# Three groups' product sums in one pair of PSUM banks per stream, with one copy out for the three

## The chip, the cores and the metric

One core of one Trainium2 chip runs the whole program. The metric is the time of the program on the device in microseconds (us); lower is better. The kernel before was timed in three runs: 1245.13, 1245.88 and 1253.26 us, median 1245.88 us.

The engines are TensorE (PE, with its weight loads as PEld), VectorE (DVE), ScalarE (ACT), GpSimd (POOL) and SyncE (SP, which issues the transfers). Each runs its own list of instructions in order, and waits at an instruction until the semaphores named there are reached.

## The reference

`x` holds 4 batches of 12608 rows of 128 numbers. Each batch is first attended to by 32 learned points, then each row attends to those 32 results, and each row goes through a small network with 1024 hidden units. All is fp32.

```python
h = mab(I, x)                       # per batch: 32 points look at all rows
x = mab(x, h)                       # each row looks at the 32 results
h = x @ w_in                        # 128 -> 1024
e = exp(h - max(h)); sm = e / (sum(e) + 1e-09)
solu = h * sm
ln = (solu - mean(solu)) / sqrt(var(solu) + 1e-06) * g_ln
out = ln @ w_out                    # 1024 -> 128
```

## The kernel before, in words

**Tiles, groups, super groups.** A batch is cut into 99 tiles of 128 rows (the last one has 64). Four tiles make a group (`GS`), so a batch has 25 groups, the last of three tiles. Three groups make a super group (`FG`), so a batch has nine: eight of three groups and one of a single group. In all there are 396 tiles, 100 groups and 36 super groups.

**The path of a tile.** PE multiplies the tile's attention weights into `h` (L946, two PSUM buffers `h0` and `h1`). DVE scales them and takes the extreme of the row (L984), ACT takes the exponential with its row sum (L994), POOL multiplies (L998), ACT squares with a row sum (L1009), and DVE transposes 32 by 32 blocks into `vt` (L1022). When the four tiles of a group are in `vt`, PE may start the group's products with the second weights (`products`, `emit` at L1067). `vt` has three buffers, and one is given back when both streams of its group have ended.

**The two streams.** The product of a group is a sum over 32 steps (`JB`) on each of four row quarters of PE. Stream 0 (`w = 0`) has quarters 0 and 1, stream 1 has quarters 2 and 3. Each stream owns two PSUM banks (`op0` for stream 0, `op1` for stream 1), one bank per quarter. A sum is 129 columns wide: 128 outputs and one column of ones. A step in which both streams put their two matmuls on PE is called a beat here. `beats` also lets one stream run beside other work that takes two quarters only: the four quarter parts of a tile's L946, and the small transposes (L550). Then the other stream stands still.

**How a stream gets on.** `products` takes the stream's only `op` buffer (L1061), and so waits until the copy of the group before it has been made. `evacuate` makes that copy (L1089): 128 x 258 numbers (two banks of 129) from PSUM into rows `i0` and `i0 + 1` of `raw`, which lies in the tile `spare`. The copy is one instruction on DVE or on ACT, whichever the planner takes. There are 200 of them: 113 on DVE, 87 on ACT.

**The end of a super group.** When all its copies are made, `finish` takes the variance from the ones' column and other sums (L1110 to L1129) and scales the rows on ACT (L1144) or on POOL (L1140); then the rows are stored.

**What sets the order.** The program is written by a list planner (`Planner`). Every step is an `Op` with an engine, a cost in ns, what it comes after, and a priority; some have an alternative on another engine (`alt`). The planner picks the next step of the engine that is free first, and so fixes the order of the instructions of each engine. A copy has the priority `t + PR_EV` with `PR_EV = -20`, which puts it ahead of the tiles' work. What the planner believes of the time decides only the order; on the chip each engine takes its list as it stands, and waits where it must.

Beside this, in the first three batches, the kernel reads the rows of the next batch and does the first attention for it (`p1`), and the second attention's weights are made some tiles ahead (`p2`). The last batch has no `p1` beside it.

Of the kernel before, what the change touches and what calls it, by code (L numbers as in the profile page):

```python
# [20 lines left out]
C = 128  # L21
# [4 lines left out]
FG = 3  # L26
PG = 12
AG = 12
JB = FF // M
# [36 lines left out]
PR_EV = -20  # L66
# [59 lines left out]
class Planner:  # L126
# [8 lines left out]
    def spawn(self, gen, prio):  # L135
        self._step([gen, prio, 0], None)
# [8 lines left out]
    def give(self, lock, buf, *after):  # L145
        lock.free.append((buf, after))
        while lock.free and lock.waiting:
            lock.waiting.sort(key=lambda w: (w[2], w[1]))
            task = lock.waiting.pop(0)[0]
            self.blocked -= 1  # L150
            self._step(task, lock.free.pop(0))
# [95 lines left out]
def set_attention_then_solu_kernel(ctx: ExitStack, tc: tile.TileContext, x, inducing, w_in, w_out, g_ln, out):  # L247
    nc = tc.nc
    NB, N, _ = x.shape
# [7 lines left out]
    start = min(FIRST, some[0][1] - 1)  # L257
    at_groups = [[(0, start), (start, some[0][1] - start)] + some[1:]] + [some] * (NB - 1)
    NP, NG = len(p1_groups), len(ff_groups)
# [15 lines left out]
    spawn, give = plan.spawn, plan.give  # L275

    def buf(shape, name, dtype=F32, where=None):
        return (where or const).tile(shape, dtype, name=name)
# [7 lines left out]
    def small(i, **widths):  # L286
# [18 lines left out]
    xT_b = buf([C, PG, P], "xT")  # L305
    H, VT, XN, XT = (Lock() for _ in range(4))
    OP = [Lock(), Lock()]
    HN, EU = Lock(hn_b[:1]), Lock()
    X2 = Lock([buf([C, AG, P], "xT2")])
    S2 = Lock([(buf([P, AG, M], f"s2_{i}"), buf([P, AG], f"mx{i}"), buf([P, AG], f"nr{i}")) for i in range(2)])  # L310
# [26 lines left out]
        out=fold[:, 0, :], in_=ident.rearrange("p (q m) -> p m q", m=M), op=ALU.add, axis=AX.X  # L337
    )
    for q in range(1, 4):
# [4 lines left out]
        out=quarter, in_=ident.rearrange("p (q m) -> p q m", m=M), op=ALU.add, axis=AX.X  # L344
# [53 lines left out]
    wc = buf([P, JB, C + 1], "wc")  # L398
# [497 lines left out]

    tiles = [(b, j, s) for b in range(NB) for j in range(NG) for s in range(ff_groups[j][1])]
    part_of = {(b, s): (k, s - s0) for b in range(NB) for k, (s0, n) in enumerate(at_groups[b]) for s in range(s0, s0 + n)}
    fin = {(b, f): dict(buf=Event(), out=[], left=2 * min(FG, NG - f * FG)) for b in range(NB) for f in range(-(-NG // FG))}
    grp = {(b, j): dict(vt=Event(), st=Event(), floor=Event(), turned=[], squared=[], over=[]) for b in range(NB) for j in range(NG)}  # L900

    def driver():
# [71 lines left out]
    def soft(t, hp, d):  # L974
# [55 lines left out]
        if len(G["turned"]) == n:  # L1030
            for w in range(2):
                spawn(products(b, j, t, w), t)
# [23 lines left out]
    def products(b, j, t, w):  # L1056

        G = grp[(b, j)]
        n = ff_groups[j][1]
        rows = n * M  # L1060
        op, rel = yield OP[w]  # L1061
        vt = G["vtb"][:, : n * FF].rearrange("p (j c) -> p j c", j=JB)
        yield wc_ready

        def emit(a, k):
            q = slice(a * M, (a + 1) * M)
            nc.tensor.matmul(op[:rows, a - 2 * w, : C + 1], lhsT=vt[q, k, :], rhs=wc[q, k, :], start=(k == 0), stop=(k == JB - 1))  # L1067

        def close(d):
            G["over"].append(d)  # L1070
            if len(G["over"]) == 2:
                give(VT, G["vtb"], *G["over"])
            spawn(evacuate(b, j, w, op, d, t + PR_EV), t + PR_EV)

        ready = max(d.end + AFTER[d.eng]["PE"] for a in (G["turned"], rel, wc_ready.after) for d in a if d is not None)
        stream[w].update(j=0, emit=emit, ready=ready, close=close, prio=t + PR_G2)
        idle = flow["idle"]
        if idle.waiting:
            plan.set(idle)

    def evacuate(b, j, w, op, dop, prio):

        F = fin[(b, j // FG)]
        rows = ff_groups[j][1] * M
        i0 = j % FG * 4 + 2 * w
        rel = yield F["buf"]

        def copied(eng):
            return lambda: eng(F["raw"][:rows, i0 : i0 + 2, :], op[:rows, :, : C + 1])  # L1089

        d = yield Op("DVE", 340, copied(nc.vector.tensor_copy), dop, rel, prio=prio, alt=Op("ACT", 265, copied(nc.scalar.copy), dop, rel, prio=prio))
        give(OP[w], op, d)
        F["out"].append(d)
        F["left"] -= 1
        if not F["left"]:
            spawn(finish(b, j // FG), prio + PR_FI)
# [91 lines left out]
    def handover():  # L1188
# [12 lines left out]
        for w in range(2):  # L1201
            give(OP[w], buf([P, 2, 512], f"op{w}", where=late), *done)
        for k in range(NP):
# [60 lines left out]
```

## Time and profile before

| | before |
|---|---|
| three runs, us | 1245.13, 1245.88, 1253.26 |
| span of the profiled execution, us | 1252.6 |
| that execution's own time, us | not given apart; of the runs, 1253.26 lies 0.7 above the span |
| PE busy, share of the span | 96% |
| DVE, ACT, POOL busy | 90%, 90%, 88% |
| mean granted clock of PE | 0.984 |
| copies out of `op` (L1089) | 113 on DVE, 87 on ACT |

Busy PE means that at least one matmul is under way. It doesn't say whether two of the four row quarters are at work or all four. So a PE that is busy for nearly the whole span can still have room, and one has to look at how full the beats are. The other three engines do one thing at a time, and their busy share is what it seems to be; short gaps between instructions are not in it.

### The profile page before, as it was taken

The numbers are of one execution on the slowest core, as the hardware profiler recorded it, in microseconds if no ns is written. First come the engines' busy times: TensorE is split into PE (matmuls) and PEld (weight loads), VectorE is DVE, ScalarE is ACT, GpSimd is POOL, SyncE is SP. The second block draws the span as 40 slices with busy tenths as digits, with TensorE's granted clock in tenths as the row PEclk, the third lists the DMA queues.
The fourth block names the chain that finished last, engine by engine and source line by source line (L and its number), as shares of the span: only waits on it lengthen the run. The fifth ranks groups of instructions, "written<-read, shape, count | busy, mean of one in ns | idle before, by whom it ended". The sixth has DMA issues, their size and how long they took to land. (4 is left out here: it accounts for less than half of the span.)

```text
span 1252.6 us, 78887 instructions
## 1 busy us (share of the span) xinstructions
PE 1200.5 (96%) x35640; PEld 1113.4 (89%) x35640; DVE 1124.9 (90%) x1816; ACT 1127.9 (90%) x2414; POOL 1101.9 (88%) x981
## 2 busy tenths in 40 slices
PE   9889999999999999999999999999999999999995
PEld 7679999999899988999898988889989999988995
DVE  5589999999999998999988987989999999999982
ACT  5479999999899998999878997989989999999994
POOL 2478899899999998999988987987999999999994
PEclk9879999999999999999999999999999999999998
DMA  9562233331224342331223231332121221211111
GB/s 355 179 170 81 80 131 105 114 101 39 86 58 133 106 130 98 81 100 61 80 80 107 64 124 55 110 110 88 57 80 56 61 56 55 55 47 45 22 31 42
DMA packets 118162, 113.68 MB, mean 91 GB/s; under 512 B 76576, under 2 KB 83776, under 8 KB 117696
## 3 DMA queue, kind: packets, MB, share of 16 engines
q1 hardware_dynamic: 117824, 108.62, 28.3%
q8 instruction: 279, 4.57, 1.5%
q14 instruction: 59, 0.48, 0.1%
HBM read 54.30 MB, written 52.18 MB: 85 GB/s over the span
## 5 line engine op out<-in xcount | busy, mean ns | idle before, releaser
L1067 PE MATMUL op<-wc,vt 32*128 32x129 f32 x25600 | 1034.2, 275 | 22.9 <-issue 16.8
L1067 PEld LDWEIGHTS op<-wc,vt 32*128 32x128 f32 x25600 | 989.5, 185 | 62.6 <-issue 48.6
L998 POOL TENSOR_TENSOR eu<-spare,eu 128x1024 f32<-128x1024 f32 x191 | 452.3, 2374 | 33.1 <-ACT eu L994 30.7
L946 PE MATMUL h<-hs,aT 32*128 32x128 f32 x6336 | 436.5, 277 | 4.9 <-DVE spare L984 1.4
L1022 DVE STREAM_TRANSPOSE vt<-eu 128x1024 f32<-128x1024 f32 x330 | 403.9, 1232 | 7.1 <-POOL eu L998 7.1
L946 PEld LDWEIGHTS h<-hs,aT 32*128 32x128 f32 x6336 | 392.2, 189 | 19.1 <-issue 4.4
L1009 ACT ACTIVATE sq<-eu 128x1024 bf16<-128x1024 f32 x330 | 346.7, 1051 | 25.4 <-POOL eu L998 20.9
L998 POOL TENSOR_TENSOR eu<-hn,eu 128x1024 f32<-128x1024 f32 x139 | 329.4, 2373 | 25.3 <-ACT eu L994 24.8
L984 DVE TENSOR_SCALAR_CACHE_REDUCE spare<-h,rn 128x1024 f32<-128x1024 f32 x227 | 285.9, 1263 | 23.3 <-PE h L946 15.8
L984 DVE TENSOR_SCALAR_CACHE_REDUCE hn<-h,rn 128x1024 f32<-128x1024 f32 x169 | 213.1, 1263 | 21.2 <-PE h L946 11.8
L994 ACT ACTIVATE eu<-spare,nm 128x1024 f32<-128x1024 f32 x191 | 217.8, 1141 | 2.9 <-DVE spare L984 2.9
L994 ACT ACTIVATE eu<-hn,nm 128x1024 f32<-128x1024 f32 x139 | 158.5, 1141 | 0.2 <-DVE hn L984 0.2
L1144 ACT ACTIVATE os<-spare,fin 128x128 f32<-128x128 f32 x272 | 85.5, 390 | 5.1 <-DMA out_dram<-os 3.6
L998 POOL TENSOR_TENSOR spare<-spare 128x1024 f32<-128x1024 f32 x36 | 85.5, 2374 | 5.2 <-ACT spare L994 5.1
L1022 DVE STREAM_TRANSPOSE vt<-spare 128x1024 f32<-128x1024 f32 x66 | 81.1, 1229 | 0.9 <-POOL spare L998 0.8
L1009 ACT ACTIVATE sq<-spare 128x1024 bf16<-128x1024 f32 x66 | 69.4, 1052 | 6.9 <-POOL spare L998 6.0
L998 POOL TENSOR_TENSOR spare<-hn,spare 128x1024 f32<-128x1024 f32 x30 | 71.2, 2372 | 2.5 <-ACT spare L994 2.3
L1089 DVE COPY spare<-op 128x258 f32<-128x258 f32 (+1 forms) x113 | 47.0, 420 | 27.4 <-PE op L1067 26.0
L1009 ACT ACTIVATION_READ_ACCUMULATOR sq<-eu 128x1 f32 x330 | 62.8, 190 | 0.0
L1089 ACT COPY spare<-op 128x258 f32<-128x258 f32 (+1 forms) x87 | 31.5, 365 | 23.9 <-PE op L1067 23.5
L550 PE MATMUL h<-ident,xn 32*128 32x32 f32 x1188 | 46.1, 220 | 1.6 <-issue 1.0
L550 PEld LDWEIGHTS h<-ident,xn 32*128 32x128 f32 x1188 | 44.4, 137 | 2.4 <-issue 1.2
(164 smaller groups left out, 1031.4 us busy)
## 6 DMA issues: line engine op xcount, KB each, us to landing
out_dram<-os SPq DMA_DIRECT2D x96, 256.0 KB, 2.6
xT<-xd SPq DMA_DIRECT2D x27, 768.0 KB, 4.9
xn<-in_x_dram SPq DMA_DIRECT2D x21, 768.0 KB, 5.4
xd<-xT SPq DMA_DIRECT2D x21, 768.0 KB, 4.1
dl<-dd SPq DMA_DIRECT2D x396, 1.0 KB, 2.8
xd<-vt SPq DMA_DIRECT2D x7, 768.0 KB, 11.5
spare<-in_x_dram SPq DMA_DIRECT2D x5, 768.0 KB, 12.8
xT<-xd SPq DMA_DIRECT2D x5, 512.0 KB, 4.7
```

The costliest lines, as they stand in the source:

```text
L550: nc.tensor.transpose(out=tr[:h, at : at + M], in_=block[rows, :h], identity=ident[rows, rows])
L946: nc.tensor.matmul(hp[:, cols], lhsT=aT[rows, i // 2, :], rhs=hs[rows, cols], start=True, stop=True)
L984: lambda: nc.vector.tensor_scalar(out=hn, in0=hp, scalar1=rn, scalar2=None, op0=ALU.mult, op1=ALU.min, accum_out=nm),
L994: "ACT", 1133, lambda: nc.scalar.activation(e, hn, AF.Exp, bias=nm, scale=-1.0, accum_out=G["S"][:, s : s + 1]), d, rel, srel,
L998: d = yield Op("POOL", 2330, lambda: nc.gpsimd.tensor_tensor(out=e, in0=hn, in1=e, op=ALU.mult), de, prio=t + PR_MU)
L1009: "ACT", 1040, lambda: nc.scalar.activation(sq, e, AF.Square, scale=1.0 / 32.0, accum_out=G["qe"][:, s, 0:1]), d,
L1022: lambda: nc.vector.transpose(out=G["vtb"][:, : n * FF].rearrange("p (j s t) -> p j s t", j=M, s=n)[:, :, s, :], in_=e.rearrange("p (a f) ...
L1067: nc.tensor.matmul(op[:rows, a - 2 * w, : C + 1], lhsT=vt[q, k, :], rhs=wc[q, k, :], start=(k == 0), stop=(k == JB - 1))
L1089: return lambda: eng(F["raw"][:rows, i0 : i0 + 2, :], op[:rows, :, : C + 1])
L1144: nc.scalar.activation(os[:rows, q, :], raw[:, q, :], AF.Copy, scale=y[:, i0 + q : i0 + q + 1])
```

## The change

The `op` buffer of a stream is now taken once per super group, by its first group, and kept by the next two. Group `i` of the super group (0, 1 or 2) writes its sums at columns `i * 129` to `i * 129 + 128` of the same two banks. A lock `TURN` keeps the groups of a stream in order. A stream that ends a group passes `TURN` on at once; only when the third group has ended is one copy made, `128 x 2 x 3 x 129`, three times as wide as before. It goes on DVE or ACT as before, and the planner's cost for it follows the width. In `raw` the rows of the two streams lie interleaved: of each block of four rows, stream 0 has the first two and stream 1 the last two. The last super group of a batch holds one group, and its copies stay as wide as they were (`96 x 258`).

```diff
+    TURN = [Lock([None]), Lock([None])]
...
-    fin = {(b, f): dict(buf=Event(), out=[], left=2 * min(FG, NG - f * FG)) for b in range(NB) for f in range(-(-NG // FG))}
+    fin = {(b, f): dict(buf=Event(), out=[], left=2, op=[None] * 2, todo=[min(FG, NG - f * FG)] * 2) for b in range(NB) for f in range(-(-NG // FG))}
...
-        op, rel = yield OP[w]
+        F, i = fin[(b, j // FG)], j % FG
+        yield TURN[w].at(b * NG + j)
+        rel = ()
+        if not i:
+            F["op"][w], rel = yield OP[w]
+        op = F["op"][w]
...
-            nc.tensor.matmul(op[:rows, a - 2 * w, : C + 1], lhsT=vt[q, k, :], rhs=wc[q, k, :], start=(k == 0), stop=(k == JB - 1))
+            nc.tensor.matmul(op[:rows, a - 2 * w, i * (C + 1) : (i + 1) * (C + 1)], lhsT=vt[q, k, :], rhs=wc[q, k, :], start=(k == 0), stop=(k == JB - 1))
...
-            spawn(evacuate(b, j, w, op, d, t + PR_EV), t + PR_EV)
+            F["todo"][w] -= 1
+            if not F["todo"][w]:
+                spawn(evacuate(b, j, w, op, d, t + PR_EV), t + PR_EV)
+            give(TURN[w], None)
...
-            return lambda: eng(F["raw"][:rows, i0 : i0 + 2, :], op[:rows, :, : C + 1])
-
-        d = yield Op("DVE", 340, copied(nc.vector.tensor_copy), dop, rel, prio=prio, alt=Op("ACT", 265, copied(nc.scalar.copy), dop, rel, prio=prio))
+            return lambda: eng(
+                F["raw"][:rows, : 4 * k, :].rearrange("p (j a) c -> p j a c", a=4)[:, :, 2 * w : 2 * w + 2].rearrange("p j a c -> p a j c"),
+                op[:rows, :, : k * (C + 1)].rearrange("p a (j c) -> p a j c", c=C + 1),
+            )
+
+        d = yield Op(
+            "DVE", 90 + 269 * k, copied(nc.vector.tensor_copy), dop, rel, prio=prio,
+            alt=Op("ACT", 90 + 215 * k, copied(nc.scalar.copy), dop, rel, prio=prio),
+        )
```

The lines of the changed kernel stand a few higher in number: L550, L654 and L946 are L551, L655 and L947 there, L1067 is L1073, and L1089 is L1098.

The planner makes a new order from this, on all engines. The change has 72 copies: 64 wide ones (37 on DVE, 27 on ACT) and 8 of the old width (6 on DVE, 2 on ACT). Three places show what moved. In the rows, a number behind a name is the buffer's; `x2` at `op` is the two matmuls of one stream in one beat.

**PE, second batch, where stream 0 goes from the first to the second group of the third super group.** Before, the last row of `op0` ahead of the long run of `op1` ends the old group, and the next one starts the new group:

```order
L1067 MATMUL op1_666<-wc_157,vt_65 128x129 x2
L550 MATMUL h1_664<-ident_138,xn0_67 128x32 x6
L1067 MATMUL op1_666<-wc_157,vt_65 128x129 x2
L550 MATMUL h1_664<-ident_138,xn0_67 128x32 x6
L1067 MATMUL op1_666<-wc_157,vt_65 128x129 x2
L1067 MATMUL op0_665<-wc_157,vt_65 128x129 x2
L1067 MATMUL op1_666<-wc_157,vt_65 128x129 x16
L1067 MATMUL op0_665<-wc_157,vt_65 128x129 x2
```

The same boundary in the change; the old group ends with the third row of `op0` and the new one starts with the next:

```order
L1073 MATMUL op0_665<-wc_157,vt_65 128x129 x2
L551 MATMUL h0_663<-ident_138,a4_93 128x32 x6
L1073 MATMUL op1_666<-wc_157,vt_65 128x129 x2
L551 MATMUL h0_663<-ident_138,a4_93 128x32 x6
L1073 MATMUL op1_666<-wc_157,vt_65 128x129 x2
L1073 MATMUL op0_665<-wc_157,vt_65 128x129 x2
L1073 MATMUL op1_666<-wc_157,vt_65 128x129 x2
L1073 MATMUL op0_665<-wc_157,vt_65 128x129 x2
L1073 MATMUL op1_666<-wc_157,vt_65 128x129 x2
L1073 MATMUL op0_665<-wc_157,vt_65 128x129 x2
L1073 MATMUL op1_666<-wc_157,vt_65 128x129 x2
```

Where stream 1 ran alone for eight steps (x16), the two streams now follow each other without a break.

**PE, second batch, where stream 0 goes from the third to the fourth super group.** Before (the first and the last row are the end of one group and the start of the next):

```order
L1067 MATMUL op0_665<-wc_157,vt_65 128x129 x2
L1067 MATMUL op1_666<-wc_157,vt_65 128x129 x2
L946 MATMUL h1_664<-hs1_125,aT0_94 128x128 x2
L1067 MATMUL op1_666<-wc_157,vt_65 128x129 x2
L946 MATMUL h1_664<-hs1_125,aT0_94 128x128 x2
L1067 MATMUL op1_666<-wc_157,vt_65 128x129 x2
L946 MATMUL h1_664<-hs1_125,aT0_94 128x128 x2
L1067 MATMUL op1_666<-wc_157,vt_65 128x129 x2
L946 MATMUL h1_664<-hs1_125,aT0_94 128x128 x2
L1067 MATMUL op1_666<-wc_157,vt_65 128x129 x2
L550 MATMUL h0_663<-ident_138,xn1_68 128x32 x6
L1067 MATMUL op0_665<-wc_157,vt_65 128x129 x2
```

And in the change:

```order
L1073 MATMUL op0_665<-wc_157,vt_65 128x129 x2
L551 MATMUL h1_664<-ident_138,xn1_68 128x32 x12
L1073 MATMUL op1_666<-wc_157,vt_65 128x129 x12
L947 MATMUL h1_664<-hs1_125,aT1_96 128x128 x2
L1073 MATMUL op1_666<-wc_157,vt_65 128x129 x2
L947 MATMUL h1_664<-hs1_125,aT1_96 128x128 x2
L1073 MATMUL op1_666<-wc_157,vt_65 128x129 x2
L947 MATMUL h1_664<-hs1_125,aT1_96 128x128 x2
L1073 MATMUL op1_666<-wc_157,vt_65 128x129 x2
L947 MATMUL h1_664<-hs1_125,aT1_96 128x128 x2
L1073 MATMUL op0_665<-wc_157,vt_65 128x129 x4
```

Between two super groups a stream still stands still, and more of the other stream's steps lie between: 9 where there were 5.

**The copies at the end of the third batch's first super group, with their waits.** Before, both were on DVE:

```order
L1089 COPY spare_66<-op1_666 128x258 [waits PE_49]
L851 STREAM_TRANSPOSE s2_0_87<-h0_663 128x384
L853 TENSOR_REDUCE mx0_88<-s2_0_87 128x12 [waits DVE_49]
L984 TENSOR_SCALAR spare_66,nm1_119<-h1_664,rn0_95 128x1024 [waits PE_49,Activation_49]
L1089 COPY spare_66<-op0_665 128x258 [waits PE_49]
```

In the change, stream 1's copy is the first of these rows on DVE:

```order
L1098 COPY spare_66<-op1_666 128x2x3x129 [waits PE_49]
L985 TENSOR_SCALAR spare_66,nm1_119<-h0_663,rn0_95 128x1024 [waits PE_49,Activation_49,Pool_49]
L869 TENSOR_REDUCE nr0_89<-a4_93 128x12
```

and stream 0's copy is on ACT:

```order
L995 ACTIVATE eu_84,st3_112<-spare_66,nm2_120 128x1024 [waits DVE_49]
L1098 COPY spare_66<-op0_665 128x2x3x129 [waits DVE_49,PE_49]
L1010 ACTIVATE sq_83,qe2_108<-eu_84 128x1024 [waits Activation_49,Pool_49]
L607 COPY xT_85<-h1_664 128x12x64 [waits DMAHW0_49,PE_49]
```

The copy on ACT now waits for DVE as well as for PE, since the two copies of a super group write interleaved rows of `raw`. Of the 36 super groups, 17 have their copies on different engines, 13 have both on DVE and 6 both on ACT.

More of the change, by code (lines that the diff above doesn't have):

```diff
@@ L1084, in evacuate @@
         rows = ff_groups[j][1] * M
-        i0 = j % FG * 4 + 2 * w
+        k = j % FG + 1
         rel = yield F["buf"]
         def copied(eng):
-            return lambda: eng(F["raw"][:rows, i0 : i0 + 2, :], op[:rows, :, : C + 1])
-        d = yield Op("DVE", 340, copied(nc.vector.tensor_copy), dop, rel, prio=prio, alt=Op("ACT", 265, copied(nc.scalar.copy), dop, rel, prio=prio))
+            return lambda: eng(
[6 more added lines that the diff above has]
+        )
         give(OP[w], op, d)
```

## The prediction

> **What bounds the kernel now.** I read the busy shares first, then the stretches, then the waits at the copies, and last single beats.
>
> ```profile
> PE 1200.5 (96%) x35640; PEld 1113.4 (89%) x35640; DVE 1124.9 (90%) x1816; ACT 1127.9 (90%) x2414; POOL 1101.9 (88%) x981
> ```
>
> Four engines stand near 90%, so the average names none of them. The stretches say more. The columns are the busy us of PE, PEld, DVE, ACT and POOL, then PE's granted clock, the transfers' share and GB/s:
>
> ```profile
> core 0: us, PE busy (x) PEld busy (x) DVE busy (x) ACT busy (x) POOL busy (x), PEclk, DMA share, GB/s
> 200.00:300.00 100.00, 99.83 (x3130) 92.50 (x3128) 96.08 (x162) 96.81 (x208) 91.16 (x74) 1.00 0.30 89
> 600.00:700.00 100.00, 94.33 (x2870) 87.38 (x2866) 90.38 (x133) 86.63 (x188) 88.75 (x80) 1.00 0.29 85
> 120.00:940.00 820.00, 801.23 (x24468) 740.72 (x24464) 763.52 (x1242) 761.03 (x1620) 742.00 (x651) 1.00 0.30 91
> 1000.00:1200.00 200.00, 195.01 (x6223) 188.91 (x6218) 191.87 (x268) 195.37 (x421) 197.07 (x168) 1.00 0.17 45
> ```
>
> In the first three batches (120 to 940) PE hardly stops (801 of 820 us), while DVE and ACT have 7% left and POOL 10%. There PE's list sets the pace, closely followed by DVE and ACT (96 and 97% at 200 to 300). In the last batch POOL is busy for 197.1 of 200 us and ACT for 195.4: POOL sets the pace, and what PE saves is worth little.
>
> PE's list is not full, though. Here a tile's L946 runs beside a stream:
>
> ```profile
> 1002.04 0.28 PE L1067 MATMUL op<-wc,vt 32*128 32x129 f32 x2
> 1002.11 0.28 PE L946 MATMUL h<-hs,aT 32*128 32x128 f32 x2
> 1002.15 0.28 PE L1067 MATMUL op<-wc,vt 32*128 32x129 f32 x2
> 1002.22 0.28 PE L946 MATMUL h<-hs,aT 32*128 32x128 f32 x2
> 1002.26 0.28 PE L1067 MATMUL op<-wc,vt 32*128 32x129 f32 x2
> ```
>
> A matmul of fp32 leaves two records, so a stream's two matmuls of one beat are four records, two such rows. The stream goes from 1002.04 to 1002.26 in one beat: 0.22 us with all four quarters at work. And here stream 1 goes alone for eight beats, the place of the x16 in the order:
>
> ```profile
> 461.62 1.84 PE L1067 MATMUL op<-wc,vt 32*128 32x129 f32 x32 [0.27 <-issue]
> 462.14 0.43 DVE L1089 COPY spare<-op 128x258 f32<-128x258 f32 x1
> ```
>
> 32 records in 1.84 us are at most 0.23 us a beat. So a beat of one stream takes as long as a beat of two and does half the work. It counts as busy all the same. The copy that stream 0 waited for was over at 462.57, and its next beat came only after the 32, since the list stands as written. The loss thus lies in the list: I counted its beats.
>
> | beats in PE's order | two streams | one stream beside L946 or L550 | one stream alone | L946 or L550 alone | sum |
> |---|---|---|---|---|---|
> | before | 2104 | 1719 | 473 | 215 | 4511 |
> | change | 2260 | 1684 | 196 | 250 | 4390 |
>
> The work is the same, and 121 beats are gone. By batch they are 29, 20, 45 and 27.
>
> **The change, part by part.** *Beats.* In the first three batches 94 beats go: 94 x 0.223 = **-21.0 us**. The 27 of the last batch would be 6.0 us, but POOL stands at 98.5% there. POOL gives up one of its 32 scalings (the change's order has 31), about 1 us by the row below; so I put **-1.0**, with 0 and -6.0 as the bounds.
>
> *The copies' work.*
>
> ```profile
> L1089 DVE COPY spare<-op 128x258 f32<-128x258 f32 x108 | 44.9, 419 | 18.0 <-PE op L1067 16.7
> L1089 ACT COPY spare<-op 128x258 f32<-128x258 f32 x84 | 30.4, 364 | 13.6 <-PE op L1067 13.3
> L606 ACT COPY xT<-h 128x768 f32<-128x768 f32 x42 | 33.0, 786 | 5.5 <-PE h L550 5.4
> L851 DVE STREAM_TRANSPOSE s<-h 128x384 f32<-128x384 f32 x27 | 15.0, 555 | 1.2 <-PE h L844 1.1
> L851 DVE STREAM_TRANSPOSE s<-h 128x256 f32<-128x256 f32 x5 | 2.2, 439 | 0.1
> L1140 POOL TENSOR_TENSOR os<-spare,fin 128x512 f32<-128x512 f32 x29 | 30.2, 1041 | 0.0
> L1144 ACT ACTIVATE os<-spare,fin 128x128 f32<-128x128 f32 x268 | 84.3, 390 | 5.1 <-DMA out_dram<-os 3.6 <-POOL fin L1129 1.3
> ```
>
> A wide copy has 774 columns. On ACT the 768-column copy from PSUM took 786 ns, so I take 0.79 us. On DVE, reads from PSUM cost (555 - 439) / 128 = 0.91 ns a column; 419 + 516 x 0.91 = 887 ns by this and at most 419 x 3 = 1257 by proportion; I take 0.93, near the first, since both rows are the same kind of reading. DVE then spends 37 x 0.93 + 6 x 0.42 = 36.9 us on copies instead of 47.0 (108 x 419 and 5 narrow ones), ACT 27 x 0.79 + 2 x 0.36 = 22.1 instead of 31.5, and takes over one scaling (4 x 0.39 = 1.6). So DVE saves 10 us and ACT 8 us of 1125. This pays for nothing in the sum by itself. It is what lets these two engines follow a PE list that is 2% shorter.
>
> *The holds.* 128 of the 198 places where a stream goes to its next group need no copy any more, and 70 are left. These hold longer: the copy itself takes 0.93 or 0.79 us instead of 0.42 or 0.36. What the holds cost PE before is in the rows of who waited for the copies:
>
> ```profile
> who waited for it (us, times):
>   PEld op L1067: 8.3, 23
>   PE op L1067: 2.1, 6
> ```
>
> The weight loads come first on PE, so 8.3 us is the loss. It is small because other work lies in between. For the change I summed, in its order, what PE has between the end of one super group and the start of the next (0.22 us for a beat, 0.85 for a p1 score by the row below), and compared it with the length of a hold.
>
> ```profile
> 817.74 0.85 PE L654 MATMUL h<-xT,indT 128*32 128x384 f32 x8
> ```
>
> With a hold of 0.8 us, 12 of the 70 places have too little work, by 3.0 us in all; with 1.1, 27 places and 9.7 us; with 1.4, 47 places and 20.7 us; with 1.9, 67 places and 50.0 us. How long is a hold beside the copy? At the end of the last batch nothing else was in the way:
>
> ```profile
> 1231.10 0.74 PE L1067 MATMUL op<-wc,vt 32*128 32x129 f32 x16
> 1231.74 0.43 DVE L1089 COPY spare<-op 128x258 f32<-128x258 f32 x1 [0.55 <-PE op L1067]
> 1231.90 0.37 ACT L1089 COPY spare<-op 128x258 f32<-128x258 f32 x1 [0.80 <-PE op L1067]
> 1232.22 0.91 PEld L1067 LDWEIGHTS op<-wc,vt 32*96 32x96 f32 x30 [0.56 <-DVE spare L1089]
> 1232.22 1.02 PE L1067 MATMUL op<-wc,vt 32*96 32x129 f32 x26 [0.37 <-DVE spare L1089]
> ```
>
> PE's last records end at 1231.84 and the next start at 1232.22, 0.38 us for copies of 0.43 and 0.37: a hold is about as long as its copy. With 0.93 and some time in the engine's queue I take 1.1 us, so 9.7 - 8.3 = **+1.5 us**.
>
> *The new wait.* In 17 super groups the second copy waits on another engine for the first, up to 0.93 us. Behind it in ACT's list stands a square (L1010 there), which nothing on POOL or DVE waits for at once, and then work that is waited for: a copy out of `h` for PE and the exponentials for POOL. Taking 0.5 us a time as the mean of none and 0.93, that is 17 x 0.5 = 8 us of ACT, which uses up what ACT saved, and of one stream; since the other stream mostly goes on, I put half on PE: **+4**, with bounds 0 and +16.
>
> *The tail.* The last hold, above, lies on the chain that ends the program. Its copies become wide: 0.93 - 0.43 = **+0.5 us**.
>
> *Unchanged.* PE's matmuls, the transfers (issue and sizes) and `finish` are the same. `finish` gets its rows half a us later; PE waits for none of that, and the last super group of the program keeps its narrow copies.
>
> Sum: -21.0 - 1.0 + 1.5 + 4 + 0.5 = **-16 us**. The profiled execution goes from a span of 1252.6 to 1236.6, and the median, 6.7 us under that span, from 1245.9 to **1230 us**. By the bounds: -21 - 6 - 8.3 = -35 (1211) if no hold costs anything, and -21 + 12.4 + 16 + 0.5 = +8 (1254) if holds last 1.4 us and every wait is paid in full.
>
> **The rivals.** *No room on the others.* PE's shorter list is followed only as far as DVE and ACT can: at 200 to 300 they have 4 and 3 us in 100. If the coupled engines were the limit, the gain is what they save: 10 us on DVE and, after the new wait, about none on ACT, so some 5 us: **1241**. For it speaks that row; against it 600 to 700, the end of the second batch and the start of the third, where all three have 9 to 13% left; 20 and 45 of the beats go in these two batches.
>
> *The holds decide.* In the change's order the two streams end a super group almost together, and 19 times both copies are on one engine, one behind the other. Then the second stream is shut for two copies, 1.9 us, and PE runs dry, as does all that waits for `h` behind it. If that were the typical hold, 50.0 - 8.3 = +42 us stand against -22: +20, **1266**. It decides from a hold of about 1.6 us on, where the loss of some 32 us eats the 22 and the 8.3 that were lost before. Against it speaks that the first of two copies still frees its stream after 0.9 us. The Trainium skill (PSUM — Partial Sum Buffer, Summary: rules for kernel authors) says to evacuate promptly, which this change does a third as often; by that rule this rival is the one to expect, and the 8.3 us that the prompt copies cost here neither bear it out nor refute it.
>
> *The copies' waits go too.* DVE and ACT stood still at copies until PE was done:
>
> ```profile
> DVE spare L1089 <- PE op L1067: 26.0, 34, 7.4
> ACT spare L1089 <- PE op L1067: 23.5, 21, 7.2
> ```
>
> Of these 49.5 us the tail has 7.4 + 7.2 + 0.55 + 0.80 = 16. Two thirds of the other 33 would go, 11 us per engine; where these engines are the ones that hold PE up, nearly one engine's share (10) comes on top of the 16, giving -26: **1220**.
>
> That the change doesn't do what it says is excluded by the order: 72 copies, 64 of them wide.
>
> **How the numbers follow.** Forecast (1230, its own range 1222 to 1237): 0.48, and four fifths of this below 1233.4, the bound of 1%. Copies' waits too (1220): 0.12. No room (1241): 0.28. Holds decide (1266): 0.12. A change of 1% is about what a measurement of this kernel can tell from none. Faster by over 1%: 0.38 + 0.12 = 0.50; within 1%: 0.10 + 0.28 = 0.38; slower by over 1%: 0.12. The range leaves out the far ends: 1213 to 1252.
>
> **What would show it.** Right: PE's busy time falls by some 20 us with the same number of records, the first three batches end about 20 us earlier and the last batch takes as long as before; the copies are 0.9 and 0.8 us long; PE's waits for copies stay under 15 us. Wrong: a wide copy of over 1.2 us; PE's waits for copies over 25 us (the holds); DVE and ACT at 97% throughout with PE waiting for `vt` (no room).

## The result, and the profile after

The changed kernel took 1255.7 us (median of 8 runs, 1253.43 to 1262.8), the kernel before 1248.6 us in the 8 runs of that series. The ratio is 1.0061, with a 95% interval of 1.004 to 1.0082: slightly slower, where 1.3% faster was forecast. Below, every ratio is to runs of the kernel before on the same chip. The profiled execution before has a span of 1252.6 us, longer than the median of 1248.6 us, so the two profiles differ by 1.8 us only, where the medians differ by 7.1 us.

The profiled execution of the change has a span of 1254.4 us. Its busy line, and two long stretches, the first as in the prediction (columns as there):

```profile
PE 1188.7 (95%) x35668; PEld 1097.1 (87%) x35668; DVE 1121.4 (89%) x1748; ACT 1124.0 (90%) x2360; POOL 1100.0 (88%) x978
```

```profile
core 0: us, PE busy (x) PEld busy (x) DVE busy (x) ACT busy (x) POOL busy (x), PEclk, DMA share, GB/s
120.00:940.00 820.00, 787.47 (x24335) 724.43 (x24331) 755.99 (x1191) 753.00 (x1571) 738.47 (x647) 0.99 0.30 92
940.00:1200.00 260.00, 250.86 (x8052) 241.73 (x8048) 247.28 (x329) 253.17 (x537) 250.07 (x223) 0.99 0.18 49
```

PE is busy 11.8 us less, DVE 3.5 and ACT 3.9, so all three have less to do, and the span is no shorter. The stretch from 120 to 940 us even holds fewer PE records than before (24335, before 24468). What PE saved has become time without work: span less busy time is 65.7 us for PE (1254.4 - 1188.7), before 52.1 (1252.6 - 1200.5), 13.6 us more. The copies themselves came out as predicted, 958 and 799 ns where 930 and 790 were taken:

```profile
L1098 DVE COPY spare<-op 128x774 f32<-128x774 f32 x37 | 35.4, 958 | 5.2 <-PE op L1073 2.8 <-ACT spare L1098 1.2 <-PE h L947 0.2
L1098 ACT COPY spare<-op 128x774 f32<-128x774 f32 x27 | 21.6, 799 | 10.6 <-DVE spare L1098 6.0 <-PE op L1073 3.4 <-PE h L551 0.8
```

The last column says what the engine waited for ahead of a copy. On ACT the largest part, 6.0 of 10.6 us, is the partner's copy on DVE. Now the waits, as us in total, times, and the longest one. Before:

```profile
PEld op L1067 <- DVE vt L1022: 3.4, 6, 0.9
ACT aT L885 <- PE h L550: 11.0, 12, 3.5
DVE spare L984 <- PE h L946: 15.8, 25, 2.5
DVE hn L984 <- PE h L946: 11.8, 14, 3.3
```

In the change:

```profile
PEld op L1073 <- DVE vt L1023: 11.3, 19, 1.1
ACT aT L886 <- PE h L551: 22.6, 19, 4.1
DVE spare L985 <- PE h L947: 22.8, 31, 3.7
DVE hn L985 <- PE h L947: 16.4, 27, 3.4
```

PE waits more for `vt` (DVE's transposes), and DVE and ACT wait more for what PE makes in `h`. Not every wait grew: POOL's for ACT's exponentials fell (from 48.3 to 42.7 us between 120 and 1200). The direct waits for the copies in the change:

```profile
who waited for it (us, times):
  PEld op L1073: 9.1, 14
  ACT spare L1098: 6.0, 7
  PE op L1073: 5.6, 12
```

PE's weight loads lost 9.1 us to copies, 8.3 before, and PE's matmuls 5.6, where it was 2.1. So the direct waits rose by 0.8 and by 3.5 us, far less than the 13.6.

The clock shows another part. PE stands still for 2.6 us here, and then gets half its clock for 3.4 us, while DVE waits 3.7 us for `h`:

```profile
500.00:505.50 5.50, 5.50 (x206) 5.50 (x206) 5.26 (x8) 5.50 (x14) 5.50 (x4) 1.00 0.37 100
505.50:508.40 2.90, 0.41 (x12) 0.21 (x5) 0.67 (x1) 2.90 (x6) 2.90 (x3) 0.99 0.52 185
508.40:511.80 3.40, 3.26 (x61) 3.26 (x64) 1.89 (x3) 0.54 (x2) 2.80 (x2) 0.50 0.09 8
```

```profile
508.54 0.37 PE L1073 MATMUL op<-wc,vt 32*128 32x129 f32 x1 [2.63 <-issue]
509.91 1.28 DVE L985 TENSOR_SCALAR_CACHE_REDUCE spare<-h,rn 128x1024 f32<-128x1024 f32 x1 [3.74 <-PE h L947]
```

The third row has the granted clock at 0.50. This is not the only fall. In the change, there are four more between 120 and 1220 us, one of them twice as long:

```profile
556.10:559.50 3.40, 3.40 (x72) 3.40 (x71) 0.78 (x2) 3.40 (x7) 2.62 (x2) 0.51 0.02 5
617.60:624.40 6.80, 6.80 (x92) 5.61 (x85) 5.61 (x6) 5.46 (x14) 6.57 (x5) 0.50 0.11 41
812.10:815.50 3.40, 3.40 (x75) 3.40 (x72) 1.84 (x4) 2.11 (x4) 3.40 (x2) 0.51 0.08 1
945.30:948.70 3.40, 3.40 (x64) 3.40 (x68) 3.02 (x4) 3.37 (x8) 2.93 (x5) 0.50 0.32 61
```

Before, there are two:

```profile
771.60:775.00 3.40, 3.40 (x71) 3.40 (x69) 2.57 (x4) 0.48 (x1) 1.68 (x1) 0.50 0.02 1
812.60:816.00 3.40, 3.40 (x79) 3.40 (x74) 0.20 (x1) 2.65 (x5) 2.01 (x1) 0.50 0.60 232
```

In all this is 20.5 us at half clock (3.41 us each, once 6.83), and 6.8 us before. PE counts as busy there, and gets through about half as much: 61 to 75 records in 3.4 us, where the row from 500 to 505.5 has 206 in 5.5 us. Half of the difference, 6.8 us, is an estimate of what the falls cost the change. In the 3.4 us ahead of each of the five falls PE had been busy for 0.9 to 1.8 us, so the waits came first. The Trainium skill (TensorE: Matmul & The Clock Gate, A second HAM failure mode: psum-queue depth-cycling) says that frequent small idle times of PE between groups of matmuls make the clock fall and rise again, at a cost in throughput. These rows agree with it, with five falls in the change.

### The profile page after: what moved, and what is told of

Read it like the earlier page. It is cut to its first block, busy times and chain, and to the rows that moved or that the text cites. A ratio compares the mean times of both kernels' runs of the same rounds, so it can differ in the third digit from the quotient of the medians.

```text
span 1254.4 us, 78805 instructions
## 1 busy us (share of the span) xinstructions
PE 1188.7 (95%) x35668; PEld 1097.1 (87%) x35668; DVE 1121.4 (89%) x1748; ACT 1124.0 (90%) x2360; POOL 1100.0 (88%) x978
## 5 line engine op out<-in xcount | busy, mean ns | idle before, releaser
L1073 PE MATMUL op<-wc,vt 32*128 32x129 f32 x25600 | 1009.1, 275 | 32.5 <-issue 19.7
L1073 PEld LDWEIGHTS op<-wc,vt 32*128 32x128 f32 x25600 | 965.1, 186 | 72.7 <-issue 49.7
L947 PE MATMUL h<-hs,aT 32*128 32x128 f32 x6336 | 441.7, 278 | 7.6 <-DVE spare L985 2.0
L947 PEld LDWEIGHTS h<-hs,aT 32*128 32x128 f32 x6336 | 398.0, 191 | 27.1 <-issue 10.6
L999 POOL TENSOR_TENSOR eu<-hn,eu 128x1024 f32<-128x1024 f32 x139 | 329.9, 2375 | 22.4 <-ACT eu L995 20.7
L1159 ACT ACTIVATE os<-spare,fin 128x128 f32<-128x128 f32 (+1 forms) x276 | 86.5, 389 | 1.2 <-POOL fin L1144 1.2
L886 ACT COPY aT<-h 128x384 f32<-128x384 f32 (+3 forms) x82 | 32.6, 408 | 22.9 <-PE h L551 22.6
L1098 DVE COPY spare<-op 128x774 f32<-128x774 f32 (+1 forms) x43 | 37.9, 882 | 13.9 <-PE op L1073 11.5
L551 PE MATMUL h<-ident,xn 32*128 32x32 f32 x1188 | 46.7, 220 | 2.2 <-issue 2.2
L551 PEld LDWEIGHTS h<-ident,xn 32*128 32x128 f32 x1188 | 44.8, 137 | 1.7 <-issue 1.7
```

Of the source, the lines that this page charges most:

```text
L551: nc.tensor.transpose(out=tr[:h, at : at + M], in_=block[rows, :h], identity=ident[rows, rows])
L886: lambda: nc.scalar.copy(in_rows(aT[:h, qa:qb, :], w), from_rows(tr, nq)[:h, qa:qb]),
L947: nc.tensor.matmul(hp[:, cols], lhsT=aT[rows, i // 2, :], rhs=hs[rows, cols], start=True, stop=True)
L999: d = yield Op("POOL", 2330, lambda: nc.gpsimd.tensor_tensor(out=e, in0=hn, in1=e, op=ALU.mult), de, prio=t + PR_MU)
L1073: nc.tensor.matmul(op[:rows, a - 2 * w, i * (C + 1) : (i + 1) * (C + 1)], lhsT=vt[q, k, :], rhs=wc[q, k, :], start=(k == 0), stop=(k == JB ...
L1098: return lambda: eng(F["raw"][:rows, : 4 * k, :].rearrange("p (j a) c -> p j a c", a=4)[:, :, 2 * w : 2 * w + 2].rearrange("p j a c -> p a ...
```

## The experiments

The kernels left one thing out or changed one thing. Two theories were held against each other. By the first, PE's list is the pace, as the prediction assumed, and the gain of its fuller beats was eaten by new waits of the wide copies. By the second, PE's list is not the pace, and beats saved there turn into waits for the others. A third came up on the way: the order that the planner makes differs by accident, and this alone moves the time.

### Is PE's list the pace? Two steps of the products less, and twice

```diff
-            nc.tensor.matmul(op[...], ..., start=(k == 0), stop=(k == JB - 1))
+            if k < JB - 2:
+                nc.tensor.matmul(op[...], ..., start=(k == 0), stop=(k == JB - 3))
```

> The kernel before, with the same order on every engine, but the last two of the 32 steps of each group's products are left out (so its sums lack 2/32 of their terms). PE has 400 of 6400 half beats less, up to 200 x 0.22 = 45 us. If PE's list sets the pace (the premise of the prediction), the time falls by 25 to 45 us. If the other engines set it, PE's saving turns into waits for vt and h, and the time falls by less than 12 us.

Measured: 0.9927 (0.9902 to 0.9952), so 9 us of 1254.0 (6 to 12).

The 45 us of the expectation are far more than this edit takes off PE's list. The two streams mostly stand at different steps, and a beat goes only when nothing is left in it. Counted in PE's order, of the 400 steps left out 233 shared a beat with a step of the other stream that stays, 112 stood beside L946 or L550, which stay, 31 stood alone, and 24 made up 12 beats of both streams. So 31 + 12 = 43 beats go, 43 x 0.223 = 9.6 us. The page has PE busy 15.0 us less than before (1200.5):

```profile
PE 1185.5 (95%) x34040; PEld 1097.4 (88%) x34040; DVE 1123.1 (90%) x1816; ACT 1126.7 (91%) x2414; POOL 1100.9 (89%) x981
```

Of 10 to 15 us that PE's list lost, some 9 came out of the time. That is most of it.

```diff
+            for r in range(2 if k >= JB - 2 else 1):
+                nc.tensor.matmul(op[...], ..., start=(k == 0), stop=(k == JB - 1 and r == 1))
```

> The kernel before, with the same order on every engine, but the last two of the 32 steps of each group's products are put on PE twice (so these terms count double in the sums). PE has up to 45 us more. If PE's list sets the pace, the time rises by 30 to 45 us. If the others set it and PE has room, it rises by less than 20 us.

Measured: 1.0408 (1.0368 to 1.0448), so 51 us, more than the most that was expected. By the same count 388 beats hold a doubled step, not 200, and PE is busy 55.4 us more:

```profile
PE 1255.9 (96%) x37240; PEld 1173.4 (90%) x37240; DVE 1128.4 (87%) x1816; ACT 1134.9 (87%) x2414; POOL 1102.2 (85%) x981
```

DVE, ACT and POOL have the same work as before and a smaller share of a longer span, so they wait more. So with the order left as it is, PE's list is paid for nearly in full when it gets longer, and for the most part when it gets shorter. The two expectations set their bounds by 45 us, and can't be read as they stand. The premise of the prediction, that PE's list sets the pace, is borne out here in the main.

### Is another engine the pace? About 40 us less on ACT, DVE and POOL

```diff
-activation(sq, e, AF.Square, ...)
+activation(sq[:, : FF - P], e[:, : FF - P], AF.Square, ...)
```

> The kernel before, same order, with ACT's squares on 896 of 1024 columns (their sums lack the rest): 396 x 128 x 0.86 ns = 43 us less work on ACT, as much as PE lost when two steps of the products were left out (which gave 9 us). If ACT sets the pace, the time falls by 25 to 43 us. If no single engine does, it falls by 5 to 15 us, as with PE.

Measured: 0.9976 (0.9948 to 1.0004).

```diff
-tensor_scalar(out=hn, in0=hp, ...)
+tensor_scalar(out=hn[:, : FF - 96], in0=hp[:, : FF - 96], ...)
```

> The kernel before, same order of the loop, with DVE's scaling of h on 928 of 1024 columns (the rest of hn holds older numbers) and three memsets ahead of the program's start: about 396 x 96 x 1.05 ns = 40 us less work on DVE. If DVE sets the pace, the time falls by 25 to 40 us. If no single engine does, by 5 to 15 us.

Measured: 0.9991 (0.9963 to 1.002).

```diff
-tensor_tensor(out=e, in0=hn, in1=e, op=ALU.mult)
+tensor_tensor(out=e[:, :976], in0=hn[:, :976], in1=e[:, :976], op=ALU.mult)
```

> The kernel before, same order, with POOL's multiplication on 976 of 1024 columns (the rest keeps the exponentials): 396 x 48 x 2.3 ns = 44 us less work on POOL. If POOL sets the pace, as it seems to in the last batch only, the time falls by 25 to 44 us, and by about 10 us if it does so in the last batch alone. If no single engine does, by 5 to 15 us.

Measured: 0.9961 (0.9929 to 0.9992). By the pages ACT is busy 35.1 us less in its run (1092.8), DVE 29.7 (1095.2) and POOL 40.1 (1061.8), and the time falls by 3, 1 and 5 us, the first two not clear of nothing. This is about a tenth of the work taken off or less, where PE brought 9 us for 10 to 15. None of these three sets the pace by itself, and PE comes nearest to it.

### The partner's wait: rows of the two streams apart

```diff
-                F["raw"][:rows, : 4 * k, :].rearrange("p (j a) c -> p j a c", a=4)[:, :, 2 * w : 2 * w + 2].rearrange("p j a c -> p a j c"),
+                F["raw"][:rows, 2 * FG * w : 2 * FG * w + 2 * k, :].rearrange("p (j a) c -> p a j c", a=2),
```

and the readers of `raw` in `finish` take the rows from there.

> The change, with the rows of the two streams in raw apart instead of interleaved; the orders of PE, DVE and POOL stay the same, and no copy waits for its partner any more. If the new wait and what it holds up ate the gain, the time falls by 8 to 20 us below the change, to 1236 to 1248. If PE's and the others' mutual waits did, it falls by 0 to 5 us, the 6.0 us that ACT's trace shows for this wait at most.

Measured: 0.9968 (0.994 to 0.9996). Against the change's 1.0061 that is 0.9%, some 11.6 us, in the range of the first theory and about twice the 6.0 us that the trace shows as ACT's wait. The order is the same on every engine. The end of the program shows the wait most plainly. The change:

```profile
1235.34 0.96 DVE L1098 COPY spare<-op 128x774 f32<-128x774 f32 x1 [0.24 <-PE op L1073]
1236.39 0.81 ACT L1098 COPY spare<-op 128x774 f32<-128x774 f32 x1 [1.39 <-DVE spare L1098]
1237.25 1.48 PEld L1073 LDWEIGHTS op<-wc,vt 32*96 32x96 f32 x52 [0.42 <-ACT spare L1098]
```

With the rows apart:

```profile
1229.28 0.97 DVE L1098 COPY spare<-op 128x774 f32<-128x774 f32 x1 [0.24 <-PE op L1073]
1229.34 0.81 ACT L1098 COPY spare<-op 128x774 f32<-128x774 f32 x1 [0.39 <-PE op L1073]
1230.53 1.70 PE L1073 MATMUL op<-wc,vt 32*96 32x129 f32 x52
```

The two copies run side by side there, and one behind the other in the change. In the change PE has both streams again 1.9 us after the first copy started (1235.34 to 1237.25), with rows apart 1.25 us after.

### As lonely as before: PE's order with the old beats

```diff
+HOLD = 900
...
+        if i:
+            ready = max(ready, F["ended"][w] + HOLD)
```

> The change, but the planner is told that a stream may go on 900 ns after its last group inside a super group too, so that PE's order has about as many lonely beats as before (4565 beats instead of 4390; before 4511), with 72 copies. If fuller beats are worth their time, this is 20 to 40 us slower than the change. If PE's list is not the pace, it is within 6 us of the change, or faster by up to 10 us, since PE stays busy, its clock falls less often and the copies' savings remain.

Measured: 1.0092 (1.0055 to 1.0129). 175 beats more than the change, 39 us of PE by the prediction's price, cost 0.3%, some 4 us, and the intervals overlap. In the profiled executions PE is busy 32.0 us more than in the change (1220.7), and without work 13.5 us less (52.2, in the change 65.7): lonely beats fill time in which PE would else have waited. This speaks for the second theory as far as beats go that a new order brings. It is one order, and the section on the accident shows what one order is worth.

### Fixed engines: copies that never stand one behind the other

```diff
+        on_dve = Op("DVE", 90 + 269 * k, ...)
+        on_act = Op("ACT", 90 + 215 * k, ...)
+        d = yield on_dve if w else on_act
```

on top of the rows apart.

> The change with the rows of the streams apart in raw, and stream 0's copies always on ACT, stream 1's always on DVE, so that the two copies of a super group never stand one behind the other (19 of 36 times they do in the change). If the holds between super groups still cost PE time, it is 3 to 8 us faster than the version with rows apart alone (ratio to before under 0.993). If they don't, it is the same or, with 7 us more on ACT, up to 4 us slower.

Measured: 0.9885 (0.984 to 0.993), 1238.0 us against 1252.3.

> The change with rows apart and fixed engines, the other way round: stream 0's copies on DVE, stream 1's on ACT (4419 beats). If two copies behind one another on one engine were what cost the time, it is as fast as with the engines the other way (ratio to before 0.984 to 0.993). If that version's order was a lucky one, it can lie anywhere between 0.984 and 1.005.

Measured: 0.987 (0.9801 to 0.994), 1237.0 us against 1252.2. The page of this one:

```profile
span 1236.1 us, 78886 instructions
PE 1189.3 (96%) x35686; PEld 1097.9 (89%) x35686; DVE 1115.6 (90%) x1737; ACT 1124.0 (91%) x2359; POOL 1101.6 (89%) x984
```

The busy times are those of the change within 6 us. What went is PE's time without work, 46.8 us where the change has 65.7, and all but one of the clock's falls between 120 and 1220 us. The same edit on the kernel before:

> The kernel before, with stream 0's copies always on ACT and stream 1's on DVE (100 each instead of 87 and 113). If the fixed engines as such, not the sharing of banks, made the version with rows apart and fixed engines 1.15% faster than before, this is 0.8 to 1.2% faster too. If it takes the sharing, this is within 0.5% of before or slower (its order has 4613 beats, 102 more).

Measured: 1.0101 (1.0039 to 1.0164). Fixed engines alone are no gain here. But PE's time without work is low in this run too (1267.0 - 1221.2 = 45.8 us, before 52.1), and PE is busy 20.7 us more, with its 102 beats more. So the loss can be that of the order, and that it takes the shared banks is not shown.

### The accident of the order

In each kind only the planner's belief of a beat was changed, which leaves the work and the rules as they are:

```diff
-BEAT = 225
+BEAT = 226
```

(or 224).

> The kernel before, with the planner's belief of a beat at 226 ns instead of 225: the same work and rules, another order (4527 beats). It shows what the accident of an order is worth: if orders of one kind lie close together, within 0.3% of before; if the accident is large, 0.5% or more away.

> The change with rows apart, planner's beat at 226 ns (4414 beats instead of 4390): as above for this kind. If orders of one kind lie close together, its ratio to before is 0.994 to 1.000, like that with 225; if the accident is large, 0.5% or more away from that.

> The kernel before, planner's beat at 224 ns (4535 beats). With 226 it was 1.1% slower than with 225. If 225 was a lucky order, this too is 0.5 to 1.5% slower than before; if 226 was an unlucky one, it is within 0.4% of before.

> The change, planner's beat at 224 ns (4401 beats). If the change's +0.6% is an accident of its order and sharing helps on average, this lies anywhere from 0.99 to 1.01 and below the mean of the before kind. If the interleaved rows cost about 0.9% whatever the order, it is about that much slower than the same order with rows apart.

> The change, planner's beat at 226 ns (4414 beats, the same orders as the version with rows apart and 226, which was at 1.0054). If the interleaved rows cost 0.9% whatever the order, this is at 1.010 to 1.018; if that cost was an accident too, within 0.4% of 1.0054.

> The change with rows apart, planner's beat at 224 ns (4401 beats, the same orders as the change with 224). If rows apart are worth 0.9%, it is that much faster than the interleaved one of this call.

> Rows apart, stream 0's copies on ACT and stream 1's on DVE, planner's beat at 224 ns (4424 beats). If fixed engines take away the copies that stand behind one another and this is worth about 1%, it is at 0.983 to 0.993 like the two orders of this kind so far. If those two were accidents, it is at 0.994 to 1.005, where the orders without fixed engines lie.

> The same with the planner's beat at 226 ns (4464 beats): same expectations. It has 74 beats more than the change; if beats were the pace, 16 us more than the version with 4390.

Measured, with the runs at 225 from above, as ratios to the kernel before:

| belief, ns | kind before | the change | rows apart | rows apart, fixed engines |
|---|---|---|---|---|
| 224 | 0.9935 (0.9905 to 0.9965) | 1.0009 (0.9986 to 1.0031) | 0.9967 (0.9942 to 0.9992) | 0.9904 (0.9872 to 0.9936) |
| 225 | 1 | 1.0061 (1.004 to 1.0082) | 0.9968 (0.994 to 0.9996) | 0.9885 (0.984 to 0.993) |
| 226 | 1.0111 (1.0041 to 1.0181) | 1.0062 (1.0035 to 1.0088) | 1.0054 (1.0025 to 1.0084) | 1.0053 (1.003 to 1.0075) |
| mean | 1.0015 | 1.0044 | 0.9996 | 0.9947 |

The kernel before at 224 is 0.65% faster than at 225, which neither of its two expectations allowed for. The pages and traces of the same kernels say more than the times. Each field has PE's time without work (span less busy time) and the time at half clock between 120 and 1220, in us, of one profiled execution each:

| belief, ns | kind before | the change | rows apart | rows apart, fixed engines |
|---|---|---|---|---|
| 224 | 47.0; 10.2 | 65.1; 17.1 | 62.3; 23.9 | 55.6; 0 |
| 225 | 52.1; 6.8 | 65.7; 20.5 | 60.6; 20.5 | 52.9; 10.2 |
| 226 | 58.0; 6.8 | 61.4; 27.3 | 59.4; 27.3 | 57.3; 34.1 |
| mean | 52.4; 7.9 | 64.1; 21.6 | 60.8; 23.9 | 55.3; 14.8 |

What follows:

- At each belief PE stands without work for longer in the change than before, by 3 to 18 us, and the clock is low for longer. On average the rows apart take away 3 us of these waits, and the fixed engines 5 to 6 more.
- Two ns in the planner's belief move the kernel before by 1.8%, and one ns by 0.6 to 1.1%. The change's 0.6% is no larger than this. At 226 the change's ratio is the lower one, with intervals that overlap. By the means, sharing the banks is worth 0.2% with rows apart and costs 0.3% with interleaved rows, both within the accident.
- The change and the rows apart have the same orders of PE at each belief. The interleaving costs 0.42, 0.93 and 0.08%, on average 0.5% or 6 us. It is on one side each time, but the 0.08% is not clear of nothing, and the size is an accident too.
- Fixed engines with shared banks are below the kind before at each belief, by 0.3 to 1.2%, and in the swapped version; at 224 and 226 the intervals overlap. At 226 this kind loses its gain as well, with the longest time at half clock of all. It is the fastest kind found; that it is so by its rule, and not in part by luck, is likely, but three beliefs and one swap are few.

## Why the prediction was wrong

**The step that failed** is the sum's account of waiting. It takes 22 us off for the beats (-21.0 and -1.0) and puts 6 us back for all waits (holds +1.5, the new wait +4, the tail +0.5), and it has no term for the clock. In the profiled pair PE's time without work rose by 13.6 us instead of 6, and its busy time fell by 11.8 us instead of 22. Together that is +1.8 us, the difference of the two spans, where -16 was forecast. So the failed terms are those for the waits, which were far too small, and the clock, which was put at nothing without a reason.

The busy time has two parts. The clock stood at half for 20.5 us and not 6.8, which cost 6.8 us by the estimate above. Without this the 121 beats took 18.6 us off PE, 0.15 us a beat and not 0.223. So of the 17.8 us between -16 and +1.8, 7.6 are waits, 6.8 are the clock and 3.4 the price of a beat. The other 5 us or so up to the medians (+7.1) lie outside this pair of profiles, and their cause stays open.

What did hold in the main is the premise. At an unchanged order 10 to 15 us less of PE's list brought 9, far more than the same from any other engine. But the change's 121 beats did not go at an unchanged order. Of the beats in which one stream stood alone, 196 were left of 473, and PE's waits grew: for `vt` to 11.3 us where it was 3.4, and for the copies. That the lonely beats had covered such waits is a reading, not shown for each place. The version with the lonely beats back fits it: PE is busy for 32.0 us more there, and without work for 13.5 us less.

**The new wait** was seen and mis-sized: +4 with a bound of 16; it is 11.6 us at this order and 6 on average of three. Rows apart, at the same orders, take it away.

**The holds** as PE's direct loss came near the forecast by the weight loads (+1.5, measured 9.1 - 8.3 = +0.8); the matmuls' own waits for copies rose by 3.5 us beside. Holds cost by another way too: copies that never stand one behind another brought 0.6, 0.8 and 0.0% in the three pairs of the last two columns. The prediction had the 19 super groups with both copies on one engine in view, and took them for a rival, not for a term.

**The tail**, +0.5, came to 1.4 (1.91 us from the first copy's start to both streams, 0.48 before: 1231.74 to 1232.22), because the partner's wait fell just there.

**The copies' work** was right in the length of a copy. The 10 and 8 us that DVE and ACT were to save came to only 3.5 and 3.9 us of busy time; the sum did not use them.

**The clock.** Across runs it goes with the time. The 8 runs of the change had a mean granted clock of 0.9774, 15 runs of the kernel before in another series 0.9817. Within those 15 a straight line gives 0.9 us for each 0.001 of clock (correlation -0.76; the slowest run, 1267.16 us, had 0.974). That would be 4 us of the difference, of the size of the 6.8 us above. The falls come behind waits and cost time in turn; what the same waits would cost at full clock, no run here separates.

**The rivals.** "No room on the others" is not borne out: DVE and ACT were busy for 92% of the stretch from 120 to 940 and not for 97%, and in the kernel before 30 to 35 us less on either brought 1 to 3 us. "The holds decide" had the direction right, and two of the three pairs above say that copies behind one another are part of the cause. But it expected 42 us of PE's waiting, and its sign, over 25 us of PE's direct waits for copies, did not come (9.1). "The copies' waits go too" saw something that came: DVE's and ACT's waits for PE ahead of copies fell from 49.5 us to 15.2 (11.5 and 3.7). But their waits for `h` in the rows above grew from 38.6 to 61.8 us in their place. None of the signs named for wrong came. Of those for right the copies' lengths and the short direct waits did; but PE's busy time fell by 11.8 us and not by some 20, and the first three batches ended 4 us later (their last copies at 989.2 us, before 985.1) and not 20 earlier. The chance of faster by over 1%, 0.50, rested on waits that were too small, and no chance was given to an accident of the order of 1% either way.

**What stays open:** why a beat less in a new order saved 0.15 us of busy time and not 0.223; how much of the change's waiting comes from the new order as such and not from the wide copies; why 226 is a bad belief in three kinds out of four (in the kinds with shared banks it has the longest time at half clock); what the waits named "issue" are (PEld 48.6 us before, 49.7 after), one of which preceded the clock's fall above; and how much of the gain of the fixed engines is their rule.

## What to carry to other kernels

A step left out of a list shortens it only where nothing else stands in the same beat: count the beats that go before you read such an experiment. Work that fills an engine's waiting time looks busy, and an order without it can bring the waits to light: compare busy time, time without work and clock apart. Where a list planner makes the order, a change of a few tenths of a percent can't be judged on one order; make several of each kind by a change that means nothing, and compare the means. When transfers out of shared buffers are merged, look at what the merged instructions write together: interleaved rows made two independent copies wait for each other, which rows apart took away for nothing.

## What the runs showed of the hardware that was not expected

In the change the granted clock fell to 0.50 for 3.4 us after an idle time of PE of 2.6 us, though PE had been busy for 5.5 of the 5.5 us before that. Of the five falls between 120 and 1220 us only this one had an idle time of over 2 us ahead of it; ahead of the others PE had been busy for 1.1 to 1.8 of 3.4 us, in shorter pieces. The falls are not in the prediction's terms.
